# Layer 2's weight chunks: the sign word made by a multiplication instead of a comparison, and the low parts of its output chunks made on GpSimd instead of VectorE

## The chip, the cores and the metric

One Trainium2 chip, one of its cores. The time is that of the core from the start of the program to its end, in microseconds (us). The kernel before was run three times: 998.94, 1000.66 and 1001.97 us, median 1000.66 us.

## What is computed

An attention with a bias that is built from a running sum, followed by two feed-forward layers over the same 2304 tokens. What matters here is the second of the two layers and the type of its weights:

```python
x = attn_out.transpose(0, 2, 1, 3).reshape(2304, 512)
h = x @ w_in; g = h * clip(h + 3, 0, 6) / 6; x = g @ w_out            # layer 1
h = x @ w_in2; g = h / (1 + exp(-h)); return (g @ w_out2).astype(float32)  # layer 2
# w_in, w_in2: 512 x 2048; w_out, w_out2: 2048 x 512; all four are float64,
# since float32 draws are multiplied by 1 / np.sqrt(...)
```

## The kernel before

**Weights.** Each weight matrix is cut into 16 chunks of 128 x 512. A chunk arrives as pairs of 32-bit words of a float64, so that low and high words alternate in the tile `raw` (`rawi` for w_in, `rawo` for w_out), and every view of one kind of word has a step of two elements, 8 bytes. The class `Chunk` turns it into float32. `fields` (lines 151 to 164) runs three instructions: ScalarE scales the low words in place (line 159) and writes the magnitude of the high words, read as float32, into a tile `mag` of the pool `stage`, of which there are three (line 160); GpSimd overwrites the high words with a sign word (line 161): it compares them with 0.0 and multiplies the 0 or 1 by -2^31, from float32 to int32. `join` (lines 166 to 177) puts the float32 together on VectorE: shift the magnitude left by 3 and OR the sign word in (line 172), add the low part (line 176).

**High and low parts.** TensorE multiplies in a rounded float32 type, so each operand is split in two: `high` rounds the value (line 182, by the helper of line 120), `low` subtracts the rounded from the exact (line 187). Every product is then three matmuls: high by high, high by low, low by high. `low("v")` runs on VectorE, `low("p")` on GpSimd.

**Feed.** The class `Feed` (lines 189 to 216) takes one chunk per tick through a pipeline: load, `fields` three ticks later, `join` one tick later, `high` and `low` another tick later. Within a tick a low part for GpSimd is written between `fields` and `join`, one for VectorE after `join`. The feed of layer 2's 16 output chunks is made in line 992, with VectorE for the low parts. Its ticks are called from `outs2`: in the loop over the last block of layer 1 (line 1191), and in the first token block of layer 2 (line 1217). Layer 2's 16 input chunks don't go through a feed; the class `Two` reads them in pairs, through the same `fields` and `join`, and forms seven combinations of each pair (lines 959 to 983), whose low parts are VectorE's (line 980).

**Layer 1's step.** For each chunk or two of chunks: the matmuls of `first` (lines 260 to 262), the gate on ScalarE and VectorE (lines 272 and 273), a rounded copy of it on GpSimd (line 276, by the helper of line 114), its low part on VectorE (line 280), and the matmuls of `second` (lines 299 to 301).

**Layer 2's step.** `step2` forms seven products of 128 x 384 for a pair (lines 1066 to 1068), adds them up on VectorE (line 1133), runs the gate on ScalarE (1125, 1126) and its low part on VectorE (1127); the matmuls of `sums2` (1083 to 1085) of the pair before run between them and read the output chunks 2q and 2q + 1 of pair q.

**Order.** The order of the instructions on each engine's queue is not that of the program text. A planner lays them out ahead of the run along a simulated time line, with the program text as priority and its own estimate of each instruction's cost. Each engine then runs its queue strictly in that order, waiting on semaphores. In the trace layer 2's first products (line 1066) stand among the matmuls of layer 1's last steps for this reason. GpSimd's queue holds the sign words, the gate copies of line 114 and nothing else from 530 us on.

Of the kernel before, what the change touches and what calls it, by code (L numbers as in the profile page):

```python
# [14 lines left out]
ALU = mybir.AluOpType  # L15
# [7 lines left out]
def f32(ap):  # L23
    return ap.bitcast(F32)
# [3 lines left out]
def kernel(  # L28
# [15 lines left out]
    nc = tc.nc  # L44
# [4 lines left out]
    NF = w1i.shape[0]  # L49
# [38 lines left out]
    def heads_of(x):  # L88
# [8 lines left out]
        out=cmask[:, NZ:], in_=cmask[:, NZ:], pattern=[[-1, P]],  # L97
# [32 lines left out]
    class Chunk:  # L130
# [20 lines left out]
        def fields(self):  # L151

            self.mag = stage.tile([P, DM], I32, tag="mag", name=f"mag{self.nm}")
            if self.src.dtype == F32:
                nc.scalar.copy(f32(self.mag), self.val)
                self.val = f32(self.mag)
                return
            low, high = self.words
            nc.scalar.activation(low, low.bitcast(U32), AF.Copy, scale=2.0**-29)
            nc.scalar.activation(f32(self.mag), f32(high), AF.Abs, scale=2.0**-112)  # L160
            nc.gpsimd.tensor_scalar(  # L161
                out=high, in0=f32(high), scalar1=0.0, scalar2=float(SIGN),
                op0=ALU.is_lt, op1=ALU.mult,
            )
# [166 lines left out]
    def bank(kind, shape, name):  # L331
# [11 lines left out]
        out=srow, in0=srow, scalar1=0.0, scalar2=1.0 / SCALE, op0=ALU.max, op1=ALU.mult  # L343
# [434 lines left out]
    feed = Feed([(kd, 0, f) for f in range(NF) for kd in "io"], "a", "v")  # L778
# [210 lines left out]
        return t  # L989

    twos = [Two(q) for q in range(NPAIR)]
    feed = Feed([("o", 1, f) for f in range(NF)], "a", "v")

    def pair(q):
        if q < NPAIR:
# [290 lines left out]
```

## Time and profile before

| | us |
|---|---|
| median of three runs | 1000.66 |
| the profiled execution | 1000.54 |
| its span, first to last instruction | 998.8 |
| TensorE busy / VectorE / ScalarE / GpSimd | 970.8 / 737.9 / 511.0 / 317.2 |

The granted TensorE clock is 0.995 of full over the span. TensorE is the engine that is nearly always busy, so a change elsewhere can only show in the time through what TensorE waits for. The stretch that the change touches lies between about 520 and 700 us: before it the attention and layer 1 run with layer 1's weights, after it all weights are ready and GpSimd has nothing left to do.

### The profile page before, as it was taken

How to read it: one execution, taken by the hardware profiler on the slowest of the kernel's cores; microseconds unless marked ns; L12 is line 12 of the kernel's file. 1: busy time of each engine (PE TensorE's matmuls, PEld its weight loads, DVE VectorE, ACT ScalarE, POOL GpSimd, SP SyncE). 2: the span in 40 equal slices, each digit the busy share in tenths (PEclk: the TensorE clock that was granted, in tenths of full speed). 3: DMA queues.
4: the chain of work that ended last, by engine and by line, in shares of the span. 5: the costliest groups of instructions: out<-in, count | busy, mean ns of one | idle time of the engine just before them, and what ended most of it. 6: DMA issues, size and time to landing. Idle time of an engine off the chain costs nothing.

```text
span 998.8 us, 17929 instructions
## 1 busy us (share of the span) xinstructions
PE 970.8 (97%) x6268; PEld 891.6 (89%) x6268; DVE 737.9 (74%) x1757; ACT 511.0 (51%) x1177; POOL 317.2 (32%) x323
## 2 busy tenths in 40 slices
PE   8899989999999999999999999999999999999997
PEld 5789979999999999999997877899988989889996
DVE  6899998888789888988866799887574434743343
ACT  6898554555455555555446656564443323432332
POOL 4457853443333443434425566532000000000000
PEclk9999999999999999999999999999999999999999
DMA  5796112312222223222215957434354233442421
GB/s 174 225 302 198 47 40 67 92 46 63 83 77 75 71 59 92 60 64 80 60 39 186 392 212 237 163 116 190 133 195 169 77 145 110 167 154 76 148 74 64
DMA packets 54419, 125.41 MB, mean 126 GB/s; under 512 B 12332, under 2 KB 34076, under 8 KB 51000
## 3 DMA queue, kind: packets, MB, share of 16 engines
q1 hardware_dynamic: 53880, 123.60, 37.3%
q8 instruction: 50, 0.82, 0.3%
q10 hardware_dynamic: 448, 0.66, 0.2%
q14 instruction: 41, 0.34, 0.1%
HBM read 99.52 MB, written 24.69 MB: 124 GB/s over the span
## 4 chain that ended last, share of the span: by engine, by line
PE 70%; DVE 11%; DMA 8%; issue 4%; POOL 4%; SPq 3%; ACT 1%; POOLq 0%; DVEq 0%; ACTq 0%
PE a L1083 6%; PE a L1084 6%; PE a L1085 6%; PE h L1066 5%; PE h L1068 5%; PE h L1067 5%; PE ph L260 4%; PE ph L261 4%; PE ph L262 4%; PE acc L299 4%; PE acc L300 4%; PE acc L301 4%; PE poB L672 4%; DMA rawi<-in_w1i_dram 3%; POOL rawo L161 2%
## 5 line engine op out<-in xcount | busy, mean ns | idle before, releaser
L260 PE MATMUL ph<-xh,wi 128*128 128x256 f32 (+1 forms) x512 | 154.1, 303 | 3.2 <-DVE g L273 3.1
L300 PE MATMUL acc<-gl,wo 128*128 128x256 f32 (+1 forms) x512 | 151.1, 297 | 2.4 <-DVE gl L280 2.4
L261 PE MATMUL ph<-xl,wi 128*128 128x256 f32 (+1 forms) x512 | 151.6, 296 | 0.0
L262 PE MATMUL ph<-xh,wi 128*128 128x256 f32 (+1 forms) x512 | 151.3, 296 | 0.0
L301 PE MATMUL acc<-gh,wo 128*128 128x256 f32 (+1 forms) x512 | 149.8, 294 | 0.0
L1125 ACT ACTIVATE gh<-h 128x384 fp32r<-128x384 f32 x96 | 50.3, 524 | 185.4 <-DVE h L1133 185.3
L299 PE MATMUL acc<-gh,wo 128*128 128x256 f32 (+1 forms) x512 | 143.8, 297 | 0.0
L1083 PE MATMUL a<-wo,gh 128*128 128x512 f32 x288 | 113.5, 394 | 1.4 <-ACT gh L1125 0.9
L1084 PE MATMUL a<-wo,gh 128*128 128x512 f32 x288 | 113.1, 393 | 0.0
L260 PEld LDWEIGHTS ph<-xh,wi 128*128 128x128 f32 x512 | 97.4, 190 | 8.9 <-DVE g L273 2.5
L300 PEld LDWEIGHTS acc<-gl,wo 128*128 128x128 f32 x512 | 96.4, 188 | 6.4 <-DVE gl L280 3.5
L262 PEld LDWEIGHTS ph<-xh,wi 128*128 128x128 f32 x512 | 97.6, 191 | 3.0
L261 PEld LDWEIGHTS ph<-xl,wi 128*128 128x128 f32 x512 | 97.5, 190 | 3.2
L301 PEld LDWEIGHTS acc<-gh,wo 128*128 128x128 f32 x512 | 96.5, 189 | 3.3
L299 PEld LDWEIGHTS acc<-gh,wo 128*128 128x128 f32 x512 | 95.6, 189 | 3.4
L161 POOL TENSOR_SCALAR rawi<-rawi 128x512 int32<-128x512 f32 x32 | 70.0, 2188 | 74.1 <-ACT magi L160 48.4
L1085 PE MATMUL a<-wo,gl 128*128 128x512 f32 x288 | 90.0, 392 | 0.0
L161 POOL TENSOR_SCALAR rawo<-rawo 128x512 int32<-128x512 f32 x32 | 74.5, 2329 | 48.0 <-ACT mago L160 46.3
L1127 DVE TENSOR_TENSOR gl<-h,gh 128x384 fp32r<-128x384 f32 x96 | 53.8, 560 | 39.9 <-ACT h L1126 38.2
L114 POOL TENSOR_SCALAR gh<-g 128x512 fp32r<-128x512 f32 x68 | 50.6, 745 | 92.6 <-DVE g L273 77.4
L1133 DVE TENSOR_TENSOR h<-h,u 128x384 f32<-128x384 f32 x72 | 40.1, 557 | 53.5 <-PE h L1068 53.2
L1066 PE MATMUL h<-x0t,w 128*128 128x384 f32 x192 | 64.9, 338 | 0.7 <-DVE u L1133 0.7
(220 smaller groups left out, 2554.6 us busy)
## 6 DMA issues: line engine op xcount, KB each, us to landing
w<-w_d SPq DMA_DIRECT2D x18, 1792.0 KB
w_d<-w SPq DMA_DIRECT2D x8, 1792.0 KB
k2B<-in_kT_dram SPq DMA_DIRECT2D x64, 144.0 KB
rawi<-in_w1i_dram SPq DMA_DIRECT2D x16, 512.0 KB
rawo<-in_w1o_dram SPq DMA_DIRECT2D x16, 512.0 KB
rawi<-in_w2i_dram SPq DMA_DIRECT2D x16, 512.0 KB
rawo<-in_w2o_dram SPq DMA_DIRECT2D x16, 512.0 KB
q2B<-in_qT_dram SPq DMA_DIRECT2D x64, 80.0 KB
```

What stands on the lines that cost most here:

```text
L161: nc.gpsimd.tensor_scalar(out=high, in0=f32(high), scalar1=0.0, scalar2=float(SIGN), op0=ALU.is_lt, op1=ALU.mult,)
L260: nc.tensor.matmul(o, wih[:, cs], xh[c], start=c == 0, stop=False)
L261: nc.tensor.matmul(o, wih[:, cs], xl[c], start=False, stop=False)
L262: nc.tensor.matmul(o, wil[:, cs], xh[c], start=False, stop=c == NDC - 1)
L299: nc.tensor.matmul(a, woh[:, cs], gh[:, jj, :], start=b0, stop=False)
L300: nc.tensor.matmul(a, woh[:, cs], gl[:, jj, :], start=False, stop=False)
L301: nc.tensor.matmul(a, wol[:, cs], gh[:, jj, :], start=False, stop=b1)
L1066: nc.tensor.matmul(ps, w[:, 0, cs], xh[:, c, :], start=c == 0, stop=False)
L1083: nc.tensor.matmul(accs[t], gh[:, k, cs], woh, start=b0, stop=False)
L1084: nc.tensor.matmul(accs[t], gh[:, k, cs], wol, start=False, stop=False)
L1085: nc.tensor.matmul(accs[t], gl[:, k, cs], woh, start=False, stop=b1)
L1127: nc.vector.tensor_tensor(out=gl[:, i, o], in0=g, in1=f32(gh[:, i, o]), op=ALU.subtract)
```

## The change

For chunks of layer 2 (`key[1]` is 1) the sign word is made by multiplying the high word, read as float32, by 0.0 and by 1.0, float32 to float32: the result is +0.0 or -0.0, whose bits are the sign word. This holds for all 32 chunks of layer 2, 16 input and 16 output chunks. And the feed of layer 2's output chunks gets "p" for "v", so that their 16 low parts go from VectorE to GpSimd, and within a tick from behind `join` to between `fields` and `join`. Layer 1's chunks keep the comparison.

```diff
@@ -158,6 +158,12 @@
             low, high = self.words
             nc.scalar.activation(low, low.bitcast(U32), AF.Copy, scale=2.0**-29)
             nc.scalar.activation(f32(self.mag), f32(high), AF.Abs, scale=2.0**-112)
+            if self.key[1]:
+                nc.gpsimd.tensor_scalar(
+                    out=f32(high), in0=f32(high), scalar1=0.0, scalar2=1.0,
+                    op0=ALU.mult, op1=ALU.mult,
+                )
+                return
             nc.gpsimd.tensor_scalar(
                 out=high, in0=f32(high), scalar1=0.0, scalar2=float(SIGN),
                 op0=ALU.is_lt, op1=ALU.mult,
@@ -989,7 +995,7 @@
         return t
 
     twos = [Two(q) for q in range(NPAIR)]
-    feed = Feed([("o", 1, f) for f in range(NF)], "a", "v")
+    feed = Feed([("o", 1, f) for f in range(NF)], "a", "p")
 
     def pair(q):
         if q < NPAIR:
```

## Rows read from the trace of the kernel before

**Rows 1.** Busy us by stretch: stretch, length, each engine (instructions), clock, DMA share, GB/s.

```profile
500.00:575.00 75.00, 74.89 (x397) 63.52 (x396) 54.12 (x103) 42.67 (x82) 31.57 (x26) 1.00 0.59 209
575.00:650.00 75.00, 70.52 (x321) 58.11 (x320) 69.04 (x109) 44.63 (x77) 45.82 (x23) 1.00 0.56 200
650.00:725.00 75.00, 75.00 (x377) 67.78 (x376) 54.20 (x98) 36.00 (x69) 15.42 (x7) 1.00 0.39 150
```

**Rows 2.** TensorE's waits in 575 to 650 us: total us, times, longest.

```profile
PE h L1066 <- DVE g L273: 1.1, 1, 1.1
PE h L1066 <- DVE h L1133: 1.0, 1, 1.0
PE a L1083 <- ACT gh L1125: 0.7, 1, 0.7
PE acc L300 <- DVE gl L280: 0.6, 1, 0.6
PE a L1083 <- DVE o L122: 0.5, 1, 0.5
PE h L1066 <- DVE u L1133: 0.4, 1, 0.4
```

**Rows 3.** TensorE's instructions around 595 us in order of time: start, us.

```profile
594.99 0.40 PE L261 MATMUL ph<-xl,wi 128*128 128x512 f32 x1
595.22 0.39 PE L262 MATMUL ph<-xh,wi 128*128 128x512 f32 x1
596.75 0.44 PE L1066 MATMUL h<-x0b,w 128*128 128x384 f32 x1 [1.14 <-DVE g L273]
```

**Rows 4.** Busy us by stretch, columns as in Rows 1, for 584 to 628.3 us.

```profile
584.00:628.30 44.30, 40.93 (x185) 33.37 (x184) 44.26 (x64) 28.91 (x50) 27.81 (x15) 1.00 0.62 214
```

**Rows 5.** VectorE's groups in 584 to 628.3 us: busy us, mean ns | idle before.

```profile
L172 DVE SCALAR_TENSOR_TENSOR mago<-mago,rawo 128x512 int32<-128x512 int32 x10 | 8.0, 798 | 1.9 <-POOL rawo L161 1.9
L176 DVE CUSTOM_DVE_ANT_0 mago<-rawo,mago 128x1024 uint16<-128x1024 uint16 x10 | 7.7, 766 | 0.0
L187 DVE TENSOR_TENSOR wo<-mago,wo 128x512 fp32r<-128x512 f32 x10 | 7.3, 726 | 0.0
...
L280 DVE TENSOR_TENSOR gl<-g,gh 128x512 fp32r<-128x512 f32 x5 | 3.8, 770 | 0.0
```

**Rows 6.** VectorE's instructions in order of time: start, us, idle time before.

```profile
584.54 1.15 DVE L187 TENSOR_TENSOR wo<-mago,wo 128x512 fp32r<-128x512 f32 x1
...
630.15 1.11 DVE L172 SCALAR_TENSOR_TENSOR mago<-mago,rawo 128x512 int32<-128x512 int32 x1 [1.89 <-POOL rawo L161]
```

**Rows 7.** The low parts of layer 2's output chunks: all, min/median/max ns, first and last start.

```profile
L187 DVE TENSOR_TENSOR wo<-mago,wo x16: 675/680/1151, 584.5 to 668.7; 128x512 fp32r<-128x512 f32 x16
```

**Rows 8.** Some GpSimd lines over the span: min/median/max ns, first and last start us.

```profile
L161 POOL TENSOR_SCALAR rawo<-rawo x32: 1990/2228/3809, 12.3 to 662.5; 128x512 int32<-128x512 f32 x32
L566 POOL TENSOR_SCALAR pb3B<-pb3B,sums x32: 685/697/1119, 132.4 to 510.0; 128x512 f32<-128x512 f32 x32
L114 POOL TENSOR_SCALAR gh<-g x68: 612/626/1198, 88.5 to 608.4; 128x512 fp32r<-128x512 f32 x68
L474 POOL TENSOR_TENSOR vsB<-vaB,vsB x32: 873/882/1655, 140.9 to 515.1; 128x320 fp32r<-128x320 f32 x32
```

**Rows 9.** GpSimd's groups in 575 to 650 us: busy us, mean ns | idle before.

```profile
L161 POOL TENSOR_SCALAR rawo<-rawo 128x512 int32<-128x512 f32 x15 | 37.2, 2482 | 22.1 <-ACT mago L160 20.4 <-PE h L1068 1.5
L114 POOL TENSOR_SCALAR gh<-g 128x512 fp32r<-128x512 f32 x6 | 5.5, 912 | 5.1 <-DVE g L273 5.1
```

**Rows 10.** The first reader of the output chunks of layer 2: min/median/max ns, first and last start.

```profile
L1083 PE MATMUL a<-wo,gh x288: 387/393/504, 621.7 to 992.6; 128*128 128x512 f32 x144
```

**Rows 11.** GpSimd's instructions in order of time: start, us, idle time before.

```profile
603.93 2.01 POOL L161 TENSOR_SCALAR rawo<-rawo 128x512 int32<-128x512 f32 x1 [2.53 <-ACT mago L160]
605.89 0.63 POOL L114 TENSOR_SCALAR gh<-g 128x512 fp32r<-128x512 f32 x1
```

**Rows 12.** VectorE's gate just ahead of that copy, in order of time: start, us.

```profile
603.67 0.68 DVE L273 SCALAR_TENSOR_TENSOR g<-g,ph 128x512 f32<-128x512 f32 x1
```

## The prediction

> **What bounds the kernel now.** I read the busy times by stretch first. Between 650 and 725 us TensorE is busy for the whole 75.00 us, and between 500 and 575 us for 74.89; between 575 and 650 us it is busy for 70.52, so that 4.48 us are idle there [rows 1]. In the same stretch VectorE is busy for 69.04 of 75 us. Most of the change's work lies in this stretch, and where TensorE is never idle the change has nothing to win. The next view is TensorE's waits in it: all six end with VectorE's results (one through ScalarE, whose gate waits for an addition of VectorE) and make up 4.3 us, the longest 1.1 us [rows 2]. The order of time adds what a stop costs beside the idle time: two matmuls of 512 columns start 0.23 us apart when nothing holds them (594.99, 595.22), while over the stop the starts are 1.53 us apart, 1.30 more for an idle time of 1.14 [rows 3]. That is 0.16 us more for each stop, some 1.0 us for six. **All that can be won here is about 4.5 + 1.0 = 5.5 us.** VectorE shows why the stops are there: from 584 to 628.3 us it is busy for 44.26 of 44.30 us [rows 4]. It works off a queue without a gap, and whatever TensorE waits for stands in that queue.
>
> **The low parts leave VectorE.** Ten of the sixteen lie in that gapless stretch and take 7.3 us of it [rows 5]; all of them run from 584.5 to 668.7 us [rows 7]. Taken out of a full queue, this is time that the results behind them come earlier. At the first stop, at 596.7 us, two of the ten stand ahead (0.68 to 1.15 us each [rows 6, 7]), which is more than the stop's 1.14 us; at the later ones more stand ahead than any stop is long.
>
> **The low parts arrive on GpSimd.** No row shows this instruction there. The nearest is the low part of the attention's v, a subtraction of two tensors of 320 elements: 882 ns median, 1655 ns at most, 873 at least [rows 8]. By elements (512/320) that is 1.4 us, which I take, and 2.6 us at the upper end; 0.9 us, the price of 320 elements, is the lower end. At the pace of ten in 44.3 us some fourteen lie between 584.5 and 650 us [rows 5, 7], which is about 20 us of GpSimd's time. TensorE's first read of a chunk is at 621.7 us [rows 10], 37 us after the first low part; a pair's two chunks are not read before its turn, and the last chunks are finished at 669 us for a seventh pair far behind. So the chunks' own lateness costs nothing; the cover is those tens of us.
>
> **The sign word.** The comparison takes 1990 ns at least, 2228 median [rows 8], and 2482 on average in the stretch [rows 9]. The multiplication isn't in the trace in this form. The upper end is what the comparison takes, 2.2 us, if the step of two elements or the write in place makes the price; the lower end is the gate copy, the same pair of operations on 512 packed elements, 626 ns; the normalisation of the attention, in place and float32 to float32, takes 697 [rows 8]. I take 0.8 us, near the latter, since operation, types and writing in place are the same and only the step differs. Fifteen signs of output chunks fall from 37.2 to 12 us, so that GpSimd, low parts included, is relieved by some 25 - 20 = 5 us of its 45.82 [rows 1, 9]. Where it matters: VectorE stands idle for 1.89 us before 630.15 us until a sign word is ready [rows 6], and then has a backlog at the last stop. That wait should go. Signs elsewhere are covered: GpSimd waited for ScalarE's magnitude for 20.4 us in the stretch [rows 9].
>
> **What is given back.** VectorE's instructions with two inputs in SBUF have two durations, about 0.68 us alone and about 1.15 when they fall together with some of GpSimd's [rows 6, 7]. In the gapless stretch the 35 instructions of the four groups shown have 2.95 us more than 35 times 0.68, beside 15 instructions of GpSimd [rows 4, 5]: 0.2 us for each of these. Ten low parts more would make that 2.0 us. The bounds are nothing (GpSimd's total time falls) and 0.47 each, 4.7 us. So VectorE's net relief in the 44.3 us is 7.3 - 2.0 = 5.3 us, at worst 2.6.
>
> The Trainium skill (GPSIMD Engine Reference, Key points) states that GpSimd shares its SBUF interfaces with VectorE and contends with its instructions that have two SBUF inputs. The two durations above agree. The same page (Engine selection) speaks against the change: an elementwise operation with two inputs belongs on VectorE, being about twice as slow on GpSimd; by it the moved part would cost an estimated 1.4 us, the value that the row of 320 elements gives too. Its pitfalls for Q7 kernels say that a read step of up to 8 bytes costs nothing extra, which no row here shows; by it the multiplication would cost no more than a packed one, and the sum would keep its sign.
>
> **The sum.** The profiled execution took 1000.54 us, 0.12 below the median of 1000.66, of which 998.8 are its span. Of the 5.5 us I take two thirds, 3.7, as won: the order of all queues is planned anew once the costs of 48 instructions change, with TensorE's products again placed close behind VectorE's results, so some stops will stand elsewhere. What is late next is TensorE itself, whose work doesn't change. **1000.54 - 3.7 = 996.8 us.**
>
> **The rivals.** *GpSimd takes it back.* The contention is at its upper end and the new plan uses up what is left, so that as many stops remain as now. For it speaks that GpSimd's new instructions have two inputs, which no instruction of the stretch on GpSimd has now; against it that net relief stays positive even at 0.47 us each. Time: 999 to 1001.5, typically 1000. *All stops go.* For it: two lows ahead of the very first stop outweigh it. Against it: the plan. Time: 995. *Slower: the gate copy queues on GpSimd.* Each step of layer 1 needs its gate copied by GpSimd before its low part and the matmuls behind it. Already now such a copy started at 605.89 us, 1.5 us after its gate ended (603.67 + 0.68), behind a sign of 603.93 [rows 11, 12]. A low part of 1.4 us, or 2.6 in contention, in front of each of some five copies would hold VectorE's low part of the gate and then TensorE by up to 5 x 1.4 = 7 us, less the 3.7 won: +3.3, 1004. It decides once sign and low part together last longer than the sign now, that is from a sign of about 1.1 us up (2.48 now, less 1.4). Against it: GpSimd's copies now wait for VectorE's gate for 5.1 us over six copies, mostly not for GpSimd [rows 9]. *The multiplication is no faster.* At 2.2 us GpSimd would have 45.8 + 20 = 66 us of work in 75 [rows 1]; the previous two rivals then apply, about 1001.
>
> **How the numbers follow.** A difference of 0.3%, 3.0 us, is about what a measurement of this kernel can tell from no change: faster is below 997.7, slower above 1003.7. Part of the stops gone, 995.5 to 998.3: 0.44, the likeliest. All gone, 994 to 995.5: 0.11. Taken back, 998.3 to 1001.5: 0.29, with the slow multiplication in it. Slower, 1001.5 to 1006: 0.16. Faster: four fifths of the first and all of the second, 0.46. Slower by over 0.3%: 0.12 of the last case. The rest, 0.42, is within. The range from 993.8 to 1002.5 leaves out about 0.05 below and 0.13 above.
>
> **What would show it.** Right: TensorE busy above 73 of the 75 us in 575 to 650; no low part of line 187 on VectorE after 530 us and sixteen on GpSimd at about 1.4 us; the sign by multiplication at about 0.8 us; VectorE with gaps between 584 and 628 us. Wrong: as many stops of TensorE as now, behind gate copies or under new names; VectorE's mean durations for lines 172 and 176 well above 0.8 us; a sign word that still takes 2 us. The prediction falls if the new order of the queues makes stops before 575 or after 650 us, where there are next to none now.

## The result and the profile after

The changed kernel takes 1012.09 us in the median of four runs (1008.73 to 1012.67), the kernel before 1001.08 (four runs, with one of 1001.50 beside the three given above): the ratio is 1.0097, with a 95% interval from 1.0073 to 1.0121. It is slower by 1%, where 996.8 us had been forecast. The profiled execution is the fastest of the four, 1008.73 us with a span of 1006.9; its span is 8.1 us longer than that of before, so that the trace accounts for 8.1 of the 11.0 us between the medians.

The busy times by stretch, columns as in [rows 1]:

```profile
500.00:575.00 75.00, 74.90 (x391) 62.67 (x390) 54.86 (x103) 41.24 (x80) 19.30 (x26) 1.00 0.58 210
575.00:650.00 75.00, 64.53 (x282) 53.49 (x281) 71.95 (x92) 45.77 (x79) 46.03 (x38) 0.95 0.52 177
650.00:725.00 75.00, 75.00 (x372) 67.11 (x371) 48.49 (x89) 33.37 (x65) 6.16 (x7) 1.00 0.37 149
```

The loss lies in the stretch where the gain was looked for; the stretches before and after it have no new stops. TensorE's idle time in 575 to 650 us rose from 4.48 to 10.47 us, 6.0 of the 8.1 us. The rest is its busy time over the span, 974.1 us against 970.8 for the same 6268 matmuls, less 1.2 us of idle time elsewhere. VectorE, which gave away its low parts, is busy for longer: 71.95 us with 92 instructions, where it was 69.04 with 109 [rows 1]. And the granted clock of TensorE is 0.95 of full there, where it was 1.00. TensorE's waits in the stretch, which answer to [rows 2] (total us, times, longest):

```profile
PE acc L306 <- DVE gl L286: 4.6, 2, 2.4
PE h L1072 <- DVE u L1139: 2.7, 1, 2.7
PE a L1091 <- DVE gl L1133: 1.1, 1, 1.1
PE acc L305 <- POOL gh L114: 1.1, 1, 1.1
PE a L1089 <- DVE o L122: 0.6, 1, 0.6
PE h L1072 <- DVE g L279: 0.4, 1, 0.4
```

Seven stops instead of six, three of them longer than 2 us, and all but one end with VectorE. Line 286 is the low part of the gate (280 before), 1139 an addition of layer 2's step (1133 before), 1133 the low part of layer 2's gate (1127). VectorE's groups in 584 to 628.3 us, against [rows 5], and the stretch itself, against [rows 4]:

```profile
L178 DVE SCALAR_TENSOR_TENSOR mago<-mago,rawo 128x512 int32<-128x512 int32 x10 | 13.0, 1300 | 0.0
L182 DVE CUSTOM_DVE_ANT_0 mago<-rawo,mago 128x1024 uint16<-128x1024 uint16 x10 | 9.5, 952 | 0.0
L286 DVE TENSOR_TENSOR gl<-g,gh 128x512 fp32r<-128x512 f32 x5 | 4.5, 897 | 0.0
```

```profile
584.00:628.30 44.30, 35.52 (x151) 28.92 (x150) 44.16 (x48) 24.72 (x42) 29.70 (x24) 0.94 0.46 159
```

The queue is as full as before (44.16 of 44.30 us), but holds 48 instructions where it held 64: the shift and OR went from 798 to 1300 ns on average, the addition from 766 to 952, the gate's low part from 770 to 897. The instructions in order of time show what does that; first VectorE, then GpSimd, then TensorE (start, us). Lines 1038 and 1042 make low parts and differences of layer 2's input, and each instruction reads two tensors:

```profile
589.73 3.33 DVE L1038 TENSOR_TENSOR x1b<-xr,x0b 128x768 fp32r<-128x768 f32 x2
592.98 2.05 DVE L1042 TENSOR_TENSOR xr<-xr,xr 128x768 f32<-128x768 f32 x1
596.00 0.68 DVE L286 TENSOR_TENSOR gl<-g,gh 128x512 fp32r<-128x512 f32 x1
```

```profile
590.25 3.96 POOL L193 TENSOR_TENSOR wo<-mago,wo 128x512 fp32r<-128x512 f32 x2
```

```profile
596.73 0.50 PE L306 MATMUL acc<-gl,wo 128*128 128x512 f32 x1 [2.40 <-DVE gl L286]
```

While GpSimd subtracts two low parts, three instructions of VectorE, which take 0.95 us each undisturbed, need 5.3 us. That is about what the five need one after another: 3 x 0.87 us, the step from start to start in e1 below, and 2 x 1.28, the least that a subtraction takes, make an estimated 5.2 us. The gate's low part comes two places behind them in VectorE's queue, and TensorE waits for it for 2.40 us. GpSimd's own lines (min/median/max ns) answer to [rows 8]: the multiplication and the low part.

```profile
L162 POOL TENSOR_SCALAR rawi<-rawi x16: 643/656/1107, 525.5 to 699.5; 128x512 f32<-128x512 f32 x16
L162 POOL TENSOR_SCALAR rawo<-rawo x16: 642/1084/1575, 572.4 to 668.5; 128x512 f32<-128x512 f32 x16
L193 POOL TENSOR_TENSOR wo<-mago,wo x16: 1277/1658/2299, 576.6 to 673.5; 128x512 fp32r<-128x512 f32 x16
```

What the long stops add beyond themselves stands in TensorE's instructions behind one of them:

```profile
603.35 0.41 PE L1072 MATMUL h<-x0t,w 128*128 128x384 f32 x1 [0.41 <-DVE g L279]
605.98 0.79 PE L306 MATMUL acc<-gl,wo 128*128 128x512 f32 x1 [2.21 <-DVE gl L286]
606.57 0.63 PE L307 MATMUL acc<-gh,wo 128*128 128x512 f32 x1
606.99 0.63 PE L306 MATMUL acc<-gl,wo 128*128 128x512 f32 x1
...
608.70 0.63 PE L306 MATMUL acc<-gl,wo 128*128 128x512 f32 x1
```

```profile
605.00:610.00 5.00, 4.02 (x11) 3.23 (x12) 5.00 (x7) 3.09 (x5) 2.10 (x2) 0.66 0.14 55
```

After 2.21 us of idle time the matmuls start 0.42 us apart instead of 0.23 [rows 3]. In 605 to 610 us the granted clock is 0.66 of full: TensorE is at 1.2 GHz instead of 2.4 for a while after the stop. From 605.98 to 608.70 there are six steps, 2.72 us where 6 x 0.23 would be 1.38: 1.3 us more.

### The profile page after: what moved, and what is told of

Read it like the earlier page. It is cut to its first block, busy times and chain, and to the rows that moved or that the text cites. A ratio compares the mean times of both kernels' runs of the same rounds, so it can differ in the third digit from the quotient of the medians.

```text
span 1006.9 us, 17929 instructions
## 1 busy us (share of the span) xinstructions
PE 974.1 (97%) x6268; PEld 893.9 (89%) x6268; DVE 742.3 (74%) x1741; ACT 511.9 (51%) x1177; POOL 292.2 (29%) x339
## 4 chain that ended last, share of the span: by engine, by line
PE 71%; DVE 13%; DMA 7%; issue 3%; SPq 3%; ACT 2%; POOL 1%; DVEq 0%; POOLq 0%; ACTq 0%
PE a L1091 6%; PE a L1089 6%; PE a L1090 6%; PE h L1072 5%; PE h L1073 5%; PE h L1074 5%; PE ph L266 4%; PE ph L267 4%; PE ph L268 4%; PE acc L305 4%; PE acc L306 4%; PE acc L307 4%; PE poB L678 3%; DMA rawi<-in_w1i_dram 2%; DMA rawi<-in_w2i_dram 2%
## 5 line engine op out<-in xcount | busy, mean ns | idle before, releaser
L286 DVE TENSOR_TENSOR gl<-g,gh 128x512 fp32r<-128x512 f32 (+1 forms) x76 | 56.3, 741 | 13.6 <-POOL gh L114 13.4
L1073 PE MATMUL h<-x1t,w 128*128 128x384 f32 x192 | 65.0, 339 | 0.0
```

The costliest lines, as they stand in the source:

```text
L286: nc.vector.tensor_tensor(out=gl, in0=g, in1=f32(gh), op=ALU.subtract)
L1073: nc.tensor.matmul(ps, w[:, 0, cs], xl[:, c, :], start=False, stop=False)
```

## The experiments

Three theories were tried against each other. **Contention**: GpSimd's subtraction, which reads two tensors, holds up VectorE's instructions that read two. **Order** (the expectations call it the plan theory): the planner, told of other operations on other engines, lays all queues out anew, and the new order makes the stops, whatever the instructions take. **Queue**: gate copies wait on GpSimd behind sign words and low parts. All ratios are to the kernel before, whose median was 1001.3 to 1001.9 us beside the experiments.

### The two halves alone, the low part with one input, and both layers

```diff
 e1_sign_only: the changed kernel, and
-    feed = Feed([("o", 1, f) for f in range(NF)], "a", "p")
+    feed = Feed([("o", 1, f) for f in range(NF)], "a", "v")
 e2_low_only: the kernel before, and
-    feed = Feed([("o", 1, f) for f in range(NF)], "a", "v")
+    feed = Feed([("o", 1, f) for f in range(NF)], "a", "p")
 e3_one_input: the changed kernel, and in low()
+            if eng == "p":
+                pool_copy(lo, self.val)
+                return
 e4_sign_all: e1, and in fields()
-            if self.key[1]:
+            if True:
```

> The sign words of layer 2 by multiplication, the low parts back on VectorE. Contention theory (GpSimd's subtraction with two inputs holds up VectorE's instructions with two inputs, about 1 us for each low part): no low part on GpSimd, so VectorE's mean for line 178 in the stretch falls from 1.16 back to 0.80 us or less, TensorE idle in 575 to 650 us at 4.5 us or less, time 997 to 1001 us. Plan theory (the queues' new order makes the stops, whatever the instructions take): the order differs from the changed kernel's in few places, so 1006 to 1012 us. Queue theory (gate copies wait on GpSimd behind sign and low part): 998 to 1001 us.

> The low parts on GpSimd, the sign words by comparison as before. Contention theory: the 16 low parts cost VectorE as much as in the changed kernel, 1008 to 1014 us, with line 172 at 1.1 us or more on average in the stretch. Plan theory: the order is nearer to that of before, 1001 to 1008 us. Queue theory: sign 2.2 us and low part 1.7 us together make the copies later than in the changed kernel, 1014 us or more, with TensorE's waits on line 300 and on the gate copy longer than 7 us.

> The changed kernel, but GpSimd makes a plain copy of the exact value with one input where it subtracted the rounded from the exact: the low parts of layer 2's output chunks hold other numbers, so this part of the computation is left out. Place in the queues and everything that waits for it stay. Contention theory: VectorE's two-input instructions are held up no more than by the gate copies, line 178 below 0.9 us on average, 996 to 1001 us. Queue theory: the instruction takes 0.65 to 1.1 us instead of 1.66, the copies wait about half as long, 1003 to 1006 us. Plan theory: 1006 to 1012 us.

> The sign words of both layers by multiplication, low parts of layer 2 on VectorE. Contention theory: as e1, and in the first 140 us, where the comparison takes 2.0 us or more on 32 chunks and TensorE loses some 25 us between its instructions, 0 to 5 us less: 993 to 1001 us. Plan theory: anywhere from 995 to 1010 us, with the stops at other places than in e1.

Measured: e1 1004.5 us, ratio 1.0032 [1.0017, 1.0047]; e2 1007.1, 1.0049 [1.0025, 1.0074]; e3 1006.0, 1.0052 [1.0029, 1.0075]; e4 1002.0, 1.0003 [0.9987, 1.0019]. No theory alone gives these four. Contention wanted no loss in e1 and e3, and both lose; the order theory wanted 1006 us or more for e1, and it falls short; the queue theory wanted 1014 us or more for e2 and 1001 at most for e1, and misses both. e3 is no clean test: its trace shows the copies waiting for VectorE's addition instead of ScalarE's rounded value, and its queues are not in the changed kernel's order. e4 differs from e1 only in layer 1's sign words, far ahead of the stretch, and has the same instructions in it, yet its ratio is 0.3% lower (the intervals just touch): the order was worth a closer look.

e1 has a stop of TensorE of 2.8 us behind a gate copy. TensorE's, GpSimd's, then VectorE's instructions around it:

```profile
594.32 2.08 PE L305 MATMUL acc<-gh,wo 128*128 128x512 f32 x4 [2.76 <-POOL gh L114]
```

```profile
590.13 4.13 POOL L114 TENSOR_SCALAR gh<-g 128x512 fp32r<-128x512 f32 x1 [5.71 <-DVE g L279]
```

```profile
589.90 0.68 DVE L182 CUSTOM_DVE_ANT_0 mago<-rawo,mago 128x1024 uint16<-128x1024 uint16 x1
590.50 0.68 DVE L193 TENSOR_TENSOR wo<-mago,wo 128x512 fp32r<-128x512 f32 x1
591.11 0.94 DVE L1042 TENSOR_TENSOR xr<-xr 128x768 f32<-128x768 f32 x1
591.98 1.81 DVE L1038 TENSOR_TENSOR x1b<-xr,x0b 128x768 fp32r<-128x768 f32 x2
594.30 1.11 DVE L286 TENSOR_TENSOR gl<-g,gh 128x512 fp32r<-128x512 f32 x1 [0.51 <-POOL gh L114]
```

A copy that takes 0.63 us in the median [rows 8] takes 4.13 here and ends at 594.26, 0.47 us after the last of five instructions of VectorE that read two inputs and stand without a gap (589.90 to 593.79). The contention runs both ways: here GpSimd is the one that is kept out, and VectorE's queue has to bring such a run just when the copy is due.

### The minimum in place of the multiplication: the same order, but not faster

With the minimum the traces show all five queues in the order of the kernel before, as if the planner priced the comparison and the minimum alike; with the multiplication they do not.

```diff
 e5_min_sign: e1, and in fields()
-                    out=f32(high), in0=f32(high), scalar1=0.0, scalar2=1.0,
-                    op0=ALU.mult, op1=ALU.mult,
+                    out=f32(high), in0=f32(high), scalar1=0.0, scalar2=0.0,
+                    op0=ALU.min, op1=ALU.mult,
 e6_min_sign_all: e5 in both layers
 e8_min_sign_low_p: e5 with the low parts on GpSimd
```

> The sign word of layer 2 as the minimum of the high word and 0.0, times 0.0, float32 to float32, low parts on VectorE. All five queues have exactly the order of the kernel before, because the planner gives the minimum the price of the comparison. Plan theory (the 0.3% of the multiplication alone comes from the new order of the queues): the instruction takes 0.65 to 1.1 us as the multiplication does, and the time is that of before or up to 3 us less, 997 to 1002 us. Rival (the fast sign word itself costs, because its accesses come closer together or because ScalarE and VectorE run ahead): 1003 to 1006 us, as with the multiplication alone.

> The minimum for the sign words of both layers, again at exactly the order of before, low parts on VectorE. Plan theory: the first 150 us, where TensorE waits for weights, get up to 5 us shorter: 993 to 1000 us. Rival: no gain there since the first weights come from memory too late anyway, 998 to 1003 us.

> The sign word by the minimum and the low parts on GpSimd, at exactly the order of the kernel with the slow sign word and the low parts on GpSimd (1007.1 us). Contention theory: the low parts' cost stays, so 1004 to 1008 us, with VectorE's line 178 at 1.0 us or more on average in 575 to 650 us. If GpSimd's queue (slow sign and low part one behind the other) was what cost: 999 to 1003 us.

Measured: e5 1002.2 us, 0.9998 [0.9984, 1.0012]; e6 1002.0, 1.0006 [0.9993, 1.0019]; e8 1004.1, 1.0031 [1.0018, 1.0043]. The premise that the minimum is quick did not hold; in e5 it takes as long as the comparison [rows 8]:

```profile
L162 POOL TENSOR_SCALAR rawo<-rawo x16: 1981/2210/3820, 574.4 to 661.6; 128x512 f32<-128x512 f32 x16
```

So e5 and e6 are the kernel before under another name, and what they show is narrower: the price hangs on the operation, not on the output's type (here float32, before int32) nor on the step of two elements (the multiplication has it too). e8, at the order of e2 and with the same instructions but for the minimum in place of the comparison, agrees with e2 within the intervals: moving the low parts beside a slow sign word costs 0.3 to 0.5%.

### The low part with the same waits, but one tensor

```diff
 e7_low_one_tensor: the changed kernel, and in low() on GpSimd
-            e.tensor_tensor(out=lo, in0=self.val, in1=f32(hi), op=ALU.subtract)
+            e.tensor_scalar(out=lo, in0=self.val, scalar1=f32(hi)[:, 0:1], scalar2=1.0,
+                            op0=ALU.mult, op1=ALU.mult)
```

> The changed kernel, but GpSimd's low part takes the rounded value as one number per partition instead of a tensor, and multiplies: it waits for the same two tiles and stands in the same place, and reads one tensor in place of two. The low parts of layer 2's output chunks hold other numbers, so this part of the computation is left out. Contention theory: the instruction takes 0.7 to 1.1 us, VectorE's line 178 falls from 1.16 to 0.9 us or less on average in 575 to 650 us, VectorE's busy time there falls below 69 us, and the time lies 4 to 6 us below the changed kernel's, 1004 to 1008 us. Plan theory alone: no less than 1009 us.

Measured 1005.5 us, 1.0043 [1.0028, 1.0059], half of the loss gone; line 178 fell from 1158 to 822 ns on average in 575 to 650 us. The order differs a little from the changed kernel's, and the instruction is shorter by itself (695 ns at least against 1277), so this alone does not separate the theories. The next ones do.

### Order and instructions taken apart

Here the program is planned with one operation, and the operation is exchanged in the finished program, so that order and waits stay exactly as planned.

```diff
 e9_mult_old_order: e5 (order of the kernel before), then
+    for fn in nc.m.functions:
+        for block in fn.blocks:
+            ins = block.instructions
+            for n in range(len(ins)):
+                i = ins[n]
+                if type(i).__name__ == "InstTensorScalarPtr" and i.op0 == ALU.min \
+                        and i.op1 == ALU.mult and i.engine == EngineType.Pool:
+                    ins[n] = copy.replace(i, op0=ALU.mult)
 e12_mult_all_old_order: the same from e6, both layers
 e10_min_new_order: e1 (order of the multiplication), its sign words exchanged for the minimum
 e11_low_copy_same_order: the changed kernel, its 16 subtractions on GpSimd exchanged for copies
```

> Layer 2's sign word by multiplication, low parts on VectorE, and every queue in exactly the order of the kernel before: the planner sees the minimum (which takes 2.0 us on GpSimd and which it prices like the comparison), and the operation is turned into the multiplication after the order is fixed. Plan theory: the order made the 0.3% of the multiplication alone, so here 997 to 1002 us, VectorE's 1.9 us waits for a sign word gone. Rival, that the fast sign word costs by itself: 1003 to 1006 us.

> As e9 with the multiplication in both layers, at exactly the order of the kernel before. Plan theory: as e9, and up to 5 us less from the first 150 us, 992 to 1002 us. Rival: the first stretch is bound by the weights' arrival and by VectorE, no gain, 998 to 1003 us.

> The reverse: the order of all queues of the kernel with the multiplication and low parts on VectorE, run with the slow minimum. Plan theory: 1004 to 1008 us. Rival, that the fast sign word costs by itself: 1000 to 1002 us.

> The changed kernel with exactly its order of all queues and its waits; after the order is fixed, GpSimd's 16 subtractions of two tensors become copies of the first, with one input. The low parts of layer 2's output chunks hold other numbers, so this part of the computation is left out. Contention theory: what is left is what the order costs, 1003 to 1007 us, VectorE's line 178 at 0.9 us or less on average in 575 to 650 us and its busy time there at 65 us or less against 72. Plan theory alone (the order makes all of the 1%): 1009 to 1013 us.

Measured: **e9 995.7 us, 0.9948 [0.9928, 0.9969]**; e12 996.1, 0.9948 [0.9930, 0.9967]; e10 1018.9, 1.0186 [1.0156, 1.0216]; e11 1004.8, 1.0029 [1.0010, 1.0048]. e9 and e1 have the same instructions (but for the second factor, 0.0 or 1.0) and differ only in order: 0.9948 against 1.0032, 0.84% or 8.4 us. The multiplication is worth 0.52% where the order is kept, and the new order is bad with either operation, worse with the slow one. e11 and the changed kernel have the same order and differ only in the subtraction: 1.0029 against 1.0097, 0.68%. e12 adds nothing to e9: layer 1's sign words at the start cost no time (TensorE is idle for 15.0 us in the first 140 us of the kernel before, not for the 25 of e4's expectation). Some of these are misses for the theories: e9 lies below the order theory's 997 to 1002 us, e10 far above its 1004 to 1008. The stretch from 575 to 650 us in e9, e11 and e10:

```profile
575.00:650.00 75.00, 73.67 (x345) 62.95 (x344) 69.89 (x112) 46.66 (x81) 25.94 (x23) 1.00 0.56 197
```

```profile
575.00:650.00 75.00, 69.11 (x309) 57.11 (x308) 68.25 (x97) 46.27 (x80) 37.69 (x41) 0.98 0.58 200
```

```profile
575.00:650.00 75.00, 66.13 (x282) 54.80 (x281) 67.22 (x100) 41.60 (x72) 45.37 (x24) 0.93 0.53 187
```

In e9 TensorE is idle for 1.33 us, in e11 for 5.89, in e10 for 8.87. In e9 VectorE still makes all low parts and is still busy for 69.89 us, but gets through 112 instructions. The shift and OR in the same stretch, in the kernel before, the changed one, e9 and e11:

```profile
L172 DVE SCALAR_TENSOR_TENSOR mago<-mago,rawo 128x512 int32<-128x512 int32 x15 | 11.8, 787 | 3.8 <-POOL rawo L161 3.8
L178 DVE SCALAR_TENSOR_TENSOR mago<-mago,rawo 128x512 int32<-128x512 int32 x14 | 16.2, 1158 | 0.7 <-POOL rawo L162 0.7
L178 DVE SCALAR_TENSOR_TENSOR mago<-mago,rawo 128x512 int32<-128x512 int32 x15 | 11.3, 754 | 1.1 <-POOL rawo L162 1.1
L178 DVE SCALAR_TENSOR_TENSOR mago<-mago,rawo 128x512 int32<-128x512 int32 x15 | 13.7, 912 | 0.7 <-POOL rawo L162 0.7
```

e11's time is what contention forecast, but VectorE's relief is smaller: 912 ns and 68.25 us busy where 900 and 65 at most were forecast. The exchange also makes GpSimd's instruction shorter (617 ns at least against 1277), so length could be the cause instead of the second input. Line 178 on the output chunks, in the changed kernel and in e11 (min/median/max ns), speaks against it:

```profile
L178 DVE SCALAR_TENSOR_TENSOR mago<-mago,rawo x32: 668/692/1783, 15.1 to 670.0; 128x512 int32<-128x512 int32 x32
L178 DVE SCALAR_TENSOR_TENSOR mago<-mago,rawo x32: 659/684/1137, 16.0 to 667.6; 128x512 int32<-128x512 int32 x32
```

In the kernel before, beside comparisons of one input that take 1.99 us and more [rows 8], the longest is 1142 ns. So on these chunks a longer instruction with one input stretched the line no further than a short one, and only the subtraction to 1.78 us.

### The whole change at the other order

```diff
 e13_mult_low_p_slow_order: e8, its sign words exchanged for the multiplication as in e9
 e14_mult_low_copy_slow_order: e13, its 16 subtractions on GpSimd exchanged for copies as in e11
```

> The whole change (multiplication, low parts on GpSimd) at the order of all queues that the planner makes when the sign word is priced like the comparison. Contention theory: the subtractions hold VectorE up by some 0.9 us each at any order, so most of the gain of e9 is lost: 1000 to 1005 us, VectorE's line 178 at 0.95 us or more on average in 575 to 650 us. Order theory (the move of the low parts costs only at the order made for the multiplication): 994 to 998 us, as e9.

> As e13 with the same order and waits, GpSimd's subtractions turned into copies with one input; the low parts of layer 2's output chunks hold other numbers, so this part of the computation is left out. Contention theory: 3 us or more below e13, 995 to 1000 us, line 178 at 0.85 us or less. Order theory: the same as e13 within 2 us.

Measured: e13 999.7 us, 0.9981 [0.9966, 0.9996]; e14 994.2, 0.9929 [0.9911, 0.9948]. The whole change, at the order planned for a slow sign word, is 0.2% faster than the kernel before; at its own order it is 1% slower. The subtraction costs 0.52% here, close to the 0.68% at the other order. e13 lies between the ranges of the two theories, next to contention's 1000 to 1005 us; e14 is the 3 us or more below it that contention asked for. VectorE's lines 178 and 182 in e13, then e14, in 575 to 650 us:

```profile
L178 DVE SCALAR_TENSOR_TENSOR mago<-mago,rawo 128x512 int32<-128x512 int32 x14 | 12.8, 915 | 0.6 <-POOL rawo L162 0.6
L182 DVE CUSTOM_DVE_ANT_0 mago<-rawo,mago 128x1024 uint16<-128x1024 uint16 x14 | 12.5, 893 | 0.1
```

```profile
L182 DVE CUSTOM_DVE_ANT_0 mago<-rawo,mago 128x1024 uint16<-128x1024 uint16 x15 | 11.8, 787 | 0.1
L178 DVE SCALAR_TENSOR_TENSOR mago<-mago,rawo 128x512 int32<-128x512 int32 x15 | 11.6, 773 | 0.6 <-POOL rawo L162 0.6
```

Over 0.68 us each these two lines have 6.3 us with subtractions and 3.0 with copies. With copies TensorE isn't idle at all in the stretch, and VectorE is busy for 64.69 us:

```profile
575.00:650.00 75.00, 75.00 (x358) 65.21 (x357) 64.69 (x100) 47.33 (x83) 32.25 (x36) 1.00 0.54 191
```

The table puts the six kernels with the multiplication side by side; the two columns on the right of a row have exactly the same order. The left one was planned with the low parts on VectorE; beside their place up to 5% of an engine's instructions stand elsewhere, so a step from it to the right is not the low parts alone.

| order planned for | low parts on VectorE | on GpSimd, subtraction | on GpSimd, copy |
|---|---|---|---|
| a slow sign word | 0.9948 (e9) | 0.9981 (e13) | 0.9929 (e14) |
| the multiplication | 1.0032 (e1) | 1.0097 (the change) | 1.0029 (e11) |

## Why the prediction was wrong

**What bounds the kernel: right.** The stretch from 575 to 650 us, VectorE's queue and some 5.5 us to win. e9 takes 5.2 us off with TensorE idle for 1.33 us. e14, whose copies are no low parts and which is therefore only an experiment, takes 7.1 us off with none, so 5.5 was somewhat low. The sign that was to bring the prediction down, stops before 575 or after 650 us, did not come.

**The sign word: the price right, its worth missed.** 0.8 us was taken, 0.65 us is what it takes undisturbed. But the sum gave it little; its gain was to be the end of a 1.89 us wait, and the low parts' departure was to bring the rest. At the old order the sign word alone brings 5.2 us (e9). The kernel before has a second such wait, which the prediction passed over, just ahead of the gapless stretch:

```profile
583.93 0.69 DVE L172 SCALAR_TENSOR_TENSOR mago<-mago,rawo 128x512 int32<-128x512 int32 x1 [1.89 <-POOL rawo L161]
```

Together they are the 3.8 us before line 172 above; in e9 1.1 us are left. That VectorE's full queue starts earlier is the likely way to TensorE's time, but no run separates it.

**The low parts leave VectorE: right in kind.** Without the second input on GpSimd, taking them off VectorE wins another 1.9 us (e14 against e9, 0.19%, within the intervals, and at an order that is not quite e9's), a part of what 7.3 us less of a full queue was to bring. **They arrive on GpSimd: about right.** 1.4 us was taken, with 2.6 as the upper end; it is 1.28 us at least, 1.66 in the median and 2.30 at most, and no stop of TensorE in the stretch waits for a chunk's low part.

**What is given back: the term that was mis-sized.** 0.2 us of VectorE's time was taken for each low part, 0.47 as the worst. In 584 to 628.3 us the 25 instructions of the three groups shown have (1300 - 680) x 10 + (952 - 680) x 10 + (897 - 680) x 5 = 10.0 us over 0.68 each, where 35 had 2.95 [rows 5]. The same three groups had 2.5 us in the kernel before. That is 7.5 us more for the ten low parts that GpSimd makes in this stretch, 0.75 us each where 0.2 was taken: as much as a low part costs on VectorE itself (0.73). Not all of it is the second input: with copies at the same order (e11) the three groups still have 6.4 us, for 29 instructions. So the relief was taken back whole, and the time that the rival "GpSimd takes it back" named from that mechanism is nearly e13's. The two steps of error: the price was averaged over GpSimd's instructions of one input, which are the only ones in the rows of this stretch, and the upper end let one instruction of VectorE be stretched once, from 0.68 to 1.15. Under a subtraction several are stretched one after the other, and line 178 to as much as 1.78. The experiments hold the order and take the second input away, and with it half of the subtraction's own time: 0.68% (e11) and 0.52% (e14).

**The sum: the step that failed most.** A third of the win was set aside because "the order of all queues is planned anew". That was the right doubt with the wrong size and sign: the new order costs 0.84% with the same instructions (e1 against e9) and 1.2% with the low parts on GpSimd (the change against e13), more than all there was to win. Along the runs e9, e1 and the change the parts are: multiplication -0.52%, order +0.84%, low parts on GpSimd +0.65% (1.0097 against 1.0032), together +0.97%. Along e9, e13 and the change they are -0.52%, low parts +0.33% and order +1.16%. So the size of a part depends on what it is added to, and the low parts' steps hold some replanning; the steps at a held order are the -0.52% (e9), the 0.68% (e11) and the 0.52% (e14).

**The rivals.** "Slower" came, and further than the 1001.5 to 1006 us of its case, but not by its mechanism. TensorE's wait for a gate copy is 1.1 us of 10.5, and the copies of the changed kernel take 623 to 1267 ns in the stretch. Nor did the copies hold up the gate's low part in 584 to 628.3 us: VectorE has no idle time before line 286 there. "GpSimd takes it back" had the mechanism of the low parts' share of the loss and stopped at zero.

**What stays open.** Which places of the new order make its stops was not separated. e1 shows one: a gate copy that VectorE's run of two-input instructions keeps out for 3.5 us. That the planner's order would be good if it knew of the contention was not tried. Why e4's order is better than e1's is open too.

## What to carry to other kernels

Where a planner fixes the order of the queues, a change of one operation is two changes; keep the order and exchange the operation alone before judging either. On GpSimd it is worth trying whether a compare or minimum in elementwise work can be a multiplication (here 0.64 us instead of 1.98), and measure before you move a subtraction of two tensors there while VectorE's queue is full of instructions with two inputs: here the time came back on VectorE. The version of e9 (or e12), multiplication at the order of the kernel before and low parts on VectorE, beats both kernels by 0.5 and 1.5%.

## What the hardware showed beyond expectation

GpSimd and VectorE's two-input instructions hold each other up in both directions, in the places shown as if they took turns. In e9 a sign word of 0.65 us takes 5.03 us:

```profile
585.33 5.03 POOL L162 TENSOR_SCALAR rawo<-rawo 128x512 f32<-128x512 f32 x1 [0.24 <-ACT mago L160]
```

and ends 0.5 us after six instructions of VectorE with two inputs that follow each other from 585.09 to 589.84 us. The Trainium skill (GPSIMD Engine Reference, Key points) names the shared SBUF interfaces and the contention with such instructions; the traces agree and add the size, a factor of up to eight for GpSimd and of 2.6 for VectorE's line 178 (0.68 to 1.78 us). One input is enough where GpSimd's instructions follow each other without a gap: at 131.44 us of the kernel before a low part on VectorE takes 2.18 us beside three of GpSimd with one tensor each. The elementwise price on GpSimd depends on the operation: 0.64 us for a multiplication of 512 elements with a step of 8 bytes, 1.98 for a minimum or a comparison.
